# A fused conv and SwiGLU stack on one core: a two-element variance step moves from ScalarE to VectorE, under a new order of steps

## Chip, cores and metric

One core of a Trainium2 chip runs the whole kernel. The metric is device microseconds (us) of one execution, the median of several runs of the compiled program; lower is better.

## The reference

The input `x` is 2048 rows by 512 features in bf16. Four blocks follow one another, A, B, A, B, each behind a layernorm and each added back to `x`:

```python
x = A_q
x = x + _A_ref(_layernorm(x), A_k, A_v, A_shift_k, A_ssm_k, A_ssm_D)   # conv block
x = x + _B_ref(_layernorm(x), B_w_gate, B_w_up, B_w_down)              # SwiGLU FFN
x = x + _A_ref(_layernorm(x), ...)                                     # same weights again
x = x + _B_ref(_layernorm(x), ...)

def _layernorm(x, axis=-1, eps=1e-5):
    m = jnp.mean(x, axis=axis, keepdims=True); v = jnp.var(x, axis=axis, keepdims=True)
    return (x - m) / jnp.sqrt(v + eps)
# _A_ref: kv = (4-tap causal shift conv of k) * v;  y = causal long conv of kv with ssm_k over
#         the 2048 positions (by FFT) + kv * ssm_D;  returns q * y, with q the normalised x
# _B_ref: (silu(q @ w_gate) * (q @ w_up)) @ w_down, 512 -> 1792 -> 512
```

The conv's output `y` does not depend on `x`, so both layers use the same `y`.

## The kernel before

The 2048 rows are cut into 4 chunks of 512 rows, and each chunk into 2 halves of 256 rows. A *unit* (layer, chunk, half) is one pass of one half through one layer: its prologue and its FFN. There are 16 units. The conv is computed chunk by chunk as DFT blocks on TensorE with spectral products on VectorE, and is interleaved with the FFNs of the units.

The **prologue** of a unit is a chain over four engines:

1. statistics of the layernorm of `x`, then `rstd = (var + eps) ** -0.5` on GpSimd (POOL), in `power()`, L891: one `tensor_tensor` with `pow` over 128x2 values. It is called here *the power step*. There are 32 of them, two in each prologue.
2. `n = (x - m) * rstd` (`normalise`, on VectorE L952 or ScalarE L947), `n *= y` (L974), `x += n` (L975), both on VectorE
3. statistics of the new `x`, the second power step, `z` normalised (L952 or L947), transposed by DMA into `zT` (L982). The FFN of the unit begins on TensorE when `zT` is there.

The statistics come in two forms. `ln_stats` uses VectorE: `bn_stats` (L900) and `bn_aggr` (L901) into `mv`; 20 of the 32 power steps read `mv`. `ln_stats_act` uses ScalarE for the sums: two `Square` activations with an accumulated sum (L924) into `sm`, then a small `Identity` activation (L928) that makes `ve = sm / D + eps` of 128x2 values; 12 of the 32 power steps read `ve`. Where ScalarE also normalises, a pair of tiny ScalarE steps (L940) or one of VectorE (L936) makes `nmr = -mean * rstd` first.

The **FFN** of a unit runs on TensorE: gate and up products into four PSUM banks `pf` (L402 in the profile, issued at L1109 and L1164), each evacuated by ScalarE (Silu into `sg`, L1111 and L1171; a cast into `hr` or `ht`, L1112 and L1175), multiplied on VectorE (L1118, L1178), transposed by DMA where the rows lie the other way (L1120), then the down product into `pd` (L1198), evacuated by ScalarE into `dn` (L1243, L1246) and added to `x` by VectorE (L1250).

The order of everything is fixed. The kernel first makes a list of 1721 steps with `add(engine, cost, emit, reads, writes, ...)`. The table `ORDER` gives each step of that list its place in one overall sequence; each engine issues its own steps in that sequence and waits on semaphores where a step needs another engine's result. A step therefore holds up everything behind it on its engine. Rings of buffers are given out along that sequence too (`pf` has 4).

Of the kernel before, what the change touches and what calls it, by code (L numbers as in the profile page):

```python
# [9 lines left out]
P = 128  # L10
F32 = mybir.dt.float32
# [3 lines left out]
ALU = mybir.AluOpType  # L15
# [314 lines left out]
def kernel(  # L330
# [58 lines left out]
    def whole(name, shape, dtype=BF16, parts=1):  # L389
        return new("one", name, shape, dtype, parts)  # L390
# [1126 lines left out]
```

## Time and profile before

| | |
|---|---|
| median of 3 runs | 341.59 us (341.46 to 341.8) |
| the profiled execution | 341.52 us, of which the span is 339.7 us |
| granted TensorE clock | 1.00 |
| busy, TensorE / VectorE / ScalarE / GpSimd | 333.5 / 299.7 / 264.2 / 35.5 us |
| instructions on the same | 2172 / 507 / 544 / 48 |
| power steps fed by `mv` (VectorE) | 20, mean 835 ns |
| power steps fed by `ve` (ScalarE) | 12, mean 1268 ns |
| ScalarE's step that makes `ve` | 12, mean 298 ns |

The span is the stretch that the profile covers; the time of an execution is 1.8 us longer. Busy time of TensorE counts a matmul to its modelled end, so idle TensorE time shows best as a gap between the starts of two matmuls.

### The profile page before, as it was taken

Reading aid. Unit: us, or ns where it says so; the run is one execution under the profiler, and the core shown is the slowest. Engines: PE = TensorE matmul, PEld = TensorE weight load, DVE = VectorE, ACT = ScalarE, POOL = GpSimd, SP = SyncE. Lnnn points to the kernel's source line nnn. Section 1 sums busy time; section 2 is a strip of 40 time slices with the busy share of each in tenths; the row PEclk is TensorE's granted clock in tenths of the full one; section 3 lists DMA queues with packets and bytes.
Section 4 is the critical chain, followed back from the end, with each engine's and each line's share of the span. In section 5 each row is a group of like instructions: output and inputs, shape, how many; then the busy total and the mean of one; then the engine's idle time right before and its main releaser. Section 6 shows DMA issues by size and latency. Waiting matters only on the chain.

```text
span 339.7 us, 5935 instructions
## 1 busy us (share of the span) xinstructions
PE 333.5 (98%) x2172; PEld 204.9 (60%) x2172; DVE 299.7 (88%) x507; ACT 264.2 (78%) x544; POOL 35.5 (10%) x48
## 2 busy tenths in 40 slices
PE   9999999799999999999999999999999999999996
PEld 7766864544545564745445464654546587858884
DVE  7899999799788999999999999999998887966465
ACT  7999999698996675979899985989675547465373
POOL 4000112303010100102110100002001000100000
PEclk9999999999999999999999999999999999999999
DMA  7999602251417445382324244420504430123011
GB/s 271 339 294 367 122 8 56 51 127 39 94 31 96 93 108 125 62 147 59 62 43 83 46 92 127 93 48 3 105 17 94 65 78 11 39 48 77 2 34 62
DMA packets 77992, 31.59 MB, mean 93 GB/s; under 512 B 69765, under 2 KB 75786, under 8 KB 77962
## 3 DMA queue, kind: packets, MB, share of 16 engines
q1 hardware_dynamic: 77808, 31.13, 39.5%
q8 instruction: 17, 0.28, 0.3%
q14 instruction: 13, 0.11, 0.1%
q10 hardware_dynamic: 154, 0.07, 0.1%
HBM read 12.33 MB, written 2.10 MB: 42 GB/s over the span
## 4 chain that ended last, share of the span: by engine, by line
PE 89%; DVE 5%; ACT 3%; POOL 1%; DMA 1%; issue 1%
PE pf L402 54%; PE pd L1198 20%; PE ps L1073 7%; PE ps L402 6%; POOL rstd L891 1%; DVE t L734 1%; PE wm L1483 1%; DVE Z L738 1%; DMA sg<-hr 1%; DVE m L875 1%; PE pt L569 0%; DVE bst L900 0%; ACT jk L924 0%; DVE G L537 0%; ACT sg L1111 0%
## 5 line engine op out<-in xcount | busy, mean ns | idle before, releaser
L402 PEld LDWEIGHTS <-zT 128*128 128x128 bf16 x528 | 51.5, 98 | 60.6 <-DMA zT<-z 1.0
L402 PE MATMUL pf<-wu_sb,zT 128*128 128x512 bf16 x264 | 65.3, 379 | 0.0
L402 PE MATMUL pf<-wg_sb,zT 128*128 128x512 bf16 x264 | 65.2, 379 | 0.0
L1198 PE MATMUL pd<-wd_sb,sg 128*128 128x512 bf16 x200 | 49.3, 379 | 0.1
L402 PE MATMUL pf<-zT,wu_sb 128*128 128x256 bf16 x368 | 46.1, 272 | 1.8 <-ACT sg L1111 1.6
L1111 ACT ACTIVATE sg<-pf 128x512 bf16<-128x512 f32 x66 | 39.2, 611 | 10.0 <-PE pf L402 8.3
L402 PE MATMUL pf<-zT,wg_sb 128*128 128x256 bf16 x368 | 46.1, 273 | 0.0
L1112 ACT CAST hr<-pf 128x512 bf16<-128x512 f32 x66 | 38.1, 598 | 8.6 <-PE pf L402 7.8
L402 PEld LDWEIGHTS <-wu_sb 128*128 128x128 bf16 x368 | 36.0, 98 | 9.8 <-issue 2.6
L744 DVE TENSOR_TENSOR t<-X,G 128x4096 bf16<-128x4096 bf16 x18 | 41.1, 2285 | 0.0
L402 PEld LDWEIGHTS <-wg_sb 128*128 128x128 bf16 x368 | 36.0, 98 | 7.3
L1175 ACT CAST ht<-pf 128x512 bf16<-128x512 f32 x46 | 26.8, 598 | 12.1 <-PE pf L402 10.1
L1198 PEld LDWEIGHTS <-sg 128*128 128x128 bf16 x200 | 19.4, 98 | 22.3 <-DMA sg<-hr 1.0
L891 POOL TENSOR_TENSOR rstd<-mv,nhalf 128x2 f32<-128x2 f32 x20 | 16.7, 835 | 150.5 <-DVE mv L901 139.5
L1171 ACT ACTIVATE sg<-pf 128x512 bf16<-128x512 f32 x46 | 27.1, 614 | 6.5 <-PE pf L402 5.7
L1198 PE MATMUL pd<-wd_sb,ht 128*128 128x512 bf16 (+1 forms) x126 | 29.9, 369 | 0.0
L891 POOL TENSOR_TENSOR rstd<-ve,nhalf 128x2 f32<-128x2 f32 x12 | 15.2, 1268 | 121.5 <-ACT ve L928 121.5
L900 DVE BATCH_NORM_STATS2 bst<-xc 128x6 f32<-128x512 bf16 x40 | 26.5, 683 | 0.6
L1178 DVE TENSOR_TENSOR ht<-ht,sg 128x512 bf16<-128x512 bf16 (+1 forms) x31 | 16.6, 546 | 9.4 <-ACT ht L1175 7.5
L1118 DVE TENSOR_TENSOR hr<-hr,sg 128x1024 bf16<-128x1024 bf16 x27 | 18.5, 685 | 5.3 <-ACT sg L1111 3.0
L511 ACT ACTIVATE X<-ps 128x512 bf16<-128x512 f32 x32 | 19.1, 614 | 1.5 <-PE ps L402 0.9
L1198 PEld LDWEIGHTS <-ht 128*128 128x128 bf16 x126 | 12.3, 98 | 12.2 <-ACT z L947 0.2
(143 smaller groups left out, 528.3 us busy)
## 6 DMA issues: line engine op xcount, KB each, us to landing
hn<-in_A_ssm_k_dram SPq DMA_DIRECT2D x4, 512.0 KB, 6.0
vt<-in_A_v_dram SPq DMA_DIRECT2D x4, 512.0 KB, 8.8
xc<-in_A_q_dram SPq DMA_DIRECT2D x4, 512.0 KB, 5.4
out_dram<-xc SPq DMA_DIRECT2D x15, 128.0 KB, 1.8
wg_sb<-in_B_w_gate_dram SPq DMA_DIRECT2D x1, 1792.0 KB
wu_sb<-in_B_w_up_dram SPq DMA_DIRECT2D x1, 1792.0 KB, 7.9
wd_sb<-in_B_w_down_dram SPq DMA_DIRECT2D x1, 1280.0 KB
sg<-hr SPq DMA_TRANSPOSE x66, 2.4
```

Source lines behind the costliest of these rows:

```text
L402: nc.tensor.matmul(o, lhsT=lhsT, rhs=rhs, start=(n == 0), stop=(n == len(terms) - 1))
L511: add("ACT", act(D), lambda: nc.scalar.activation(out=view(), in_=ps.t[:], func=ACT.Copy, scale=scale), r=[ps], w=[(buf, keys)], conv=conv)
L744: dve(8 * D, lambda t=t, part=part: nc.vector.tensor_mul(out=t.t[:], in0=x.t[:, :, part:part + 1, :].to_broadcast((P, R, 2, D)), in1=g.t[: ...
L891: add("POOL", cost, lambda: nc.gpsimd.tensor_tensor(out=rstd.t[:], in0=var(), in1=nhalf.t[:].to_broadcast((P, n)), op=ALU.pow), r=reads + ...
L900: add("DVE", 0.6, lambda st=st, i=i: nc.vector.bn_stats(out=st.t[:, 0:6], in_=xs[c].t[:, i, :]), r=[(xs[c], (i,))], w=[st])
L1073: nc.tensor.matmul(bank.t[:, half_ * C:(half_ + 1) * C], lhsT=lhsT(i), rhs=rhs(i), start=(first and i == 0 and half_ == 0), stop=(last and ...
L1111: add("ACT", act(D), lambda ps=ps, dst=dst, o=o, which=which: nc.scalar.activation(out=rows(dst, o), in_=ps.t[:], func=ACT.Silu) if which ...
L1112: out=rows(dst, o), in_=ps.t[:], func=ACT.Silu) if which == "g" else nc.scalar.copy(out=rows(dst, o), in_=ps.t[:]),
L1118: dve(n * W, lambda: nc.vector.tensor_mul(out=hr.t[:], in0=hr.t[:], in1=sg.t[:]), [sg], [hr], due=(unit, k / pairs, 0.0, "h"))
L1171: add("ACT", act(D), lambda ps=ps, o=o, sg=sg: nc.scalar.activation(out=sg.t[:, o:o + 2, :], in_=ps.t[:], func=ACT.Silu), r=[ps], w=[(sg, ...
L1175: add("ACT", act(D), lambda ps=ps, o=o, ht=ht: nc.scalar.copy(out=ht.t[:, o:o + 2, :], in_=ps.t[:]), r=[ps], w=[(ht, (o // 2,))], due=(uni ...
L1198: nc.tensor.matmul((pds[o] if not cs.start else pds[HP]).t[:, cs], lhsT=ht.tiles(q, o), rhs=wt["d"].t[:, ft, cs], start=(ft == std0 and no ...
```

## The change

`ve` is no longer made by ScalarE with an activation whose bias is a tile holding eps, but by VectorE with one `tensor_scalar` (multiply by 1/D, add eps). The tile `eps` and the GpSimd memset that filled it go away, so there are 1720 steps, and every power step now reads a value that VectorE wrote. The table `ORDER` is another permutation throughout.

```diff
@@ ORDER: all 1721 entries replaced by 1720 others @@
-    6, 53, 44, 124, 2, 7, 4, 12, 24, 1, 3, 0, 17, 18, 30, 10, 8, 11, 9, 15, 27, 21, 19, 16, 20, ...
+    4, 44, 184, 2, 0, 1, 6, 20, 7, 8, 14, 16, 17, 18, 5, 3, 9, 10, 12, 26, 15, 21, 13, 19, 22, ...
...
-    eps = whole("eps", [P, 1], F32)
...
         ve = new("ve", "ve", [P, n], F32)
-        add("ACT", TINY, lambda: nc.scalar.activation(out=ve.t[:], in_=sm.t[:, n:2 * n], func=ACT.Identity, scale=1.0 / D, bias=eps.t[:]),
-            r=[(sm, range(n, 2 * n)), eps], w=[ve])
+        add("DVE", 0.08, lambda: nc.vector.tensor_scalar(out=ve.t[:], in0=sm.t[:, n:2 * n], scalar1=1.0 / D, scalar2=LN_EPS,
+                                                         op0=ALU.mult, op1=ALU.add), r=[(sm, range(n, 2 * n))], w=[ve])
         return nm, power(lambda: ve.t[:], [ve], n, PWA)
...
-    add("POOL", 0.1, lambda: nc.gpsimd.memset(eps.t[:], LN_EPS), w=[eps], due=-47)
```

What the new table says on VectorE around four of the places that the prediction speaks of (`VE` is the new step; each list is the order of issue):

| prologue | before | after |
|---|---|---|
| unit (0,0,0), first power step | ..., L537, L539, L537, L734, L734, L734, L738, ... | ..., L537, L539, L734, L734, `VE`, L738, L734, ... |
| unit (1,0,0), first power step | L920, L1250, L649, L649, L748, L744, L1118, L744, L1118, L974 | L920, L1250, L748, L649, L638, `VE`, L638, L649, L1118, L744, L1118, L901, L974 |
| unit (1,1,1), first power step | L920, L1250, L900, L744, L748, L1118, L748, L974 | L920, L1250, L744, `VE`, L744, L1118, L748, L974 |
| unit (1,1,1), second power step | L974, L975, L901, L900, L900, L901, L901, L1118, L952, L936 | L974, L975, L1118, L900, L900, L901, L901, L748, L936 |

128 rows, old and new, of the table ORDER are left out of this document.

## The prediction

> **What bounds the kernel now.** The page comes first, for the engine that is never idle, then the stages, for where it is idle after all.
>
> ```profile
> PE 333.5 (98%) x2172; PEld 204.9 (60%) x2172; DVE 299.7 (88%) x507; ACT 264.2 (78%) x544; POOL 35.5 (10%) x48
> ```
>
> ```profile
> 30.00:40.00 10.00, 9.41 (x90) 7.78 (x88) 9.52 (x16) 9.53 (x26) 1.64 (x2) 1.00 0.99 245
> 50.00:60.00 10.00, 10.00 (x52) 4.95 (x51) 9.96 (x13) 9.85 (x22) 2.42 (x1) 1.00 0.27 54
> 60.00:70.00 10.00, 8.20 (x57) 5.33 (x56) 7.50 (x12) 7.32 (x15) 3.38 (x2) 1.00 0.33 66
> 190.00:200.00 10.00, 10.00 (x60) 5.69 (x59) 9.97 (x14) 9.71 (x18) 1.40 (x1) 1.00 0.32 66
> ```
>
> The columns are the stretch, its length, then busy time of PE, PEld, DVE, ACT and POOL, the granted clock and DMA. TensorE is full nearly everywhere at clock 1.00. The change takes nothing from TensorE, so it can only gain what TensorE waits for, and the one large hole lies at 60 to 70 us. The chain of waits names its cause, and the timeline shows it at work:
>
> ```profile
> 57.21 0.30 ACT ve L928
> 57.59 5.04 POOL rstd L891
> 62.65 0.30 ACT nmr L940
> ```
>
> ```profile
> 56.98 2.28 DVE L744 TENSOR_TENSOR t<-X,G 128x4096 bf16<-128x4096 bf16 x1
> 57.59 5.03 POOL L891 TENSOR_TENSOR rstd<-ve,nhalf 128x2 f32<-128x2 f32 x1 [10.93 <-ACT ve L928]
> 59.18 0.69 DVE L1118 TENSOR_TENSOR hr<-hr,sg 128x1024 bf16<-128x1024 bf16 x1
> 59.78 2.29 DVE L744 TENSOR_TENSOR t<-X,G 128x4096 bf16<-128x4096 bf16 x1
> 62.57 0.38 PE L402 MATMUL ps<-hs,fwd 128*128 128x512 bf16 x1
> 64.51 1.03 PE L402 MATMUL pf<-zT,wu_sb 128*128 128x256 bf16 x8 [1.56 <-ACT sg L1111]
> 65.69 1.03 PE L402 MATMUL pf<-zT,wu_sb 128*128 128x256 bf16 x8 [0.15 <-ACT sg L1171]
> 66.56 3.01 PE L1198 MATMUL pd<-wd_sb,sg 128*128 128x512 bf16 x12
> ```
>
> This is the first power step of unit (1,0,0). ScalarE released it in the middle of a VectorE product (56.98 to 59.26); it came through only 0.55 us after VectorE had fallen idle at 62.07, past two boundaries between instructions. ScalarE stood at nmr until 62.65, the Silu evacuations behind that were late, and TensorE ran out of `pf` banks.
>
> In full flow a 512-column matmul starts every 0.215 us and a 256-column one every 0.109, as the rows of 12 and 8 show with their last matmul's 0.38 and 0.27 taken off. By that, TensorE waited 64.51 - 62.57 - 0.21 = 1.73, then 65.69 - 64.51 - 0.87 = 0.31, then 0.25 inside the row of 12: **2.3 us**.
>
> **The change part by part.**
>
> ```profile
> L891 POOL TENSOR_TENSOR rstd<-mv,nhalf 128x2 f32<-128x2 f32 x20 | 16.7, 835 | 150.5 <-DVE mv L901 139.5
> L891 POOL TENSOR_TENSOR rstd<-ve,nhalf 128x2 f32<-128x2 f32 x12 | 15.2, 1268 | 121.5 <-ACT ve L928 121.5
> L928 ACT ACTIVATE ve<-sm,eps 128x2 f32<-128x2 f32 x12 | 3.6, 298 | 0.2
> L920 DVE SCALAR_TENSOR_TENSOR nm<-sm,mv 128x2 f32<-128x2 f32 x4 | 0.6, 156 | 0.3 <-ACT dn L1246 0.3
> L1263 POOL MEMSET eps<- 128x1 f32 x1 | 0.1, 93 | 0.0
> 45.46 0.65 DVE L1178 TENSOR_TENSOR ht<-ht,sg 128x1024 bf16<-128x1024 bf16 x1
> 45.62 1.03 POOL L891 TENSOR_TENSOR rstd<-mv,nhalf 128x2 f32<-128x2 f32 x1 [6.36 <-DVE mv L901]
> 46.02 2.28 DVE L744 TENSOR_TENSOR t<-X,G 128x4096 bf16<-128x4096 bf16 x1
> ```
>
> *Removed:* twelve ScalarE steps, 12 x 0.298 = 3.6 us, and a memset of 0.09 us that nobody waits for. Both lie beside TensorE's work: zero on the path, and a loss is excluded; a gain is the first rival.
>
> *Added:* twelve VectorE steps. The nearest row is L920, of the same 128x2 values: 12 x 0.156 = 1.9 us of VectorE, beside TensorE's work except in the start.
>
> *The power step itself.* A power step released by VectorE is not free of VectorE. At 45.46 VectorE had already gone on to its next instruction when the step started at 45.62; the step ended at 46.65, 0.54 us after that instruction (46.11), although a 2.28 us product followed at 46.02. So it waits for one VectorE instruction, whichever the order puts behind the trigger, and then gets through. Behind `mv` in the old order that instruction is short, hence the mean of 835 ns.
>
> The Trainium skill says the same more sharply (SBUF — State Buffer, "Who interferes with whom"): an instruction of VectorE with two SBUF inputs and one of GpSimd that reads SBUF exclude each other, and the first to issue blocks the other for its whole length. That speaks against this change, since VectorE now always issues first. By that rule the step at 57.59 would have come free at 59.26; the trace has 2.8 us more.
>
> *Unit (1,0,0).* In the new table the 0.69 us L638 follows the new step, so the power step should take about 1.0 as at 45.62, where it took 5.03. VectorE's other work ahead of L974 is no longer than before. The 2.3 us go, and next late is nothing: the chain that made `zT` too late becomes about 4 us shorter, more than TensorE waited. **-2.3 us.**
>
> *Start.* The first VE step stands in a VectorE chain that ends in TensorE's waits before the first FFN (0.6 us in the 30 to 40 row). It adds 0.156 us there, and up to 0.3 if it waits for ScalarE's square: **+0.2 us**.
>
> *Unit (1,1,1).* Here the new table puts a 2.28 us product (L744) right behind the new step.
>
> ```profile
> 150.72 1.03 PE L402 MATMUL pf<-wu_sb,zT 128*128 128x512 bf16 x4
> 151.43 0.16 DVE L920 SCALAR_TENSOR_TENSOR nm<-sm,mv 128x2 f32<-128x2 f32 x1 [0.34 <-ACT dn L1246]
> 154.69 0.84 POOL L891 TENSOR_TENSOR rstd<-ve,nhalf 128x2 f32<-128x2 f32 x1 [11.74 <-ACT ve L928]
> 155.64 0.59 ACT L1112 CAST hr<-pf 128x512 bf16<-128x512 f32 x1
> 156.76 1.22 DVE L748 TENSOR_TENSOR t<-t,t 128x2048 bf16<-128x2048 bf16 x1
> 158.04 0.69 DVE L974 TENSOR_TENSOR n<-n,Yk 128x1024 bf16<-128x1024 bf16 x1
> 160.93 0.69 DVE L1118 TENSOR_TENSOR hr<-hr,sg 128x1024 bf16<-128x1024 bf16 x1
> 161.16 1.66 POOL L891 TENSOR_TENSOR rstd<-mv,nhalf 128x2 f32<-128x2 f32 x2 [1.15 <-DVE mv L901]
> 162.20 0.16 DVE L936 SCALAR_TENSOR_TENSOR nmr<-mv,rstd 128x2 f32<-128x2 f32 x1 [0.26 <-POOL rstd L891]
> 162.41 1.50 ACT L947 ACTIVATE z<-xc,nmr,rstd 128x512 bf16<-128x512 bf16 x2
> 166.68 1.03 PE L402 MATMUL pf<-wu_sb,zT 128*128 128x512 bf16 x4
> ```
>
> ```profile
> sg<-hr SPq DMA_TRANSPOSE x66, 2.4
> ```
>
> I count from 150.72, where TensorE begins unit (1,1,0). Before: L920 at 0.7, power step done at 4.8, L974 at 7.3, nmr at 11.5, first z done at 12.5 (half of the 1.50), `zT` 2.4 later at 14.9, used at 16.0.
>
> After: L920 at 0.7, L1250 (0.69) and one L744 (2.28) ahead of the new step, which so starts at 3.6; the second L744 runs from 3.7 to 6.0, the power step ends at 6.5 (+0.55). From there to L974 the rows have 2.5, of which ScalarE spent 0.5 finishing a cast; ScalarE is free now: L974 at 8.5. Up to nmr the rows have 4.2; the new order adds an L1118 in this stretch (0.6 from start to start) and has the L748 (1.22) behind the trigger where the L1118 (0.69) was, but nothing is late ahead of it otherwise: 8.5 + 4.2 + 0.6 + 0.5 = 13.8 to 13.9. First z done at 14.9, `zT` at 17.3.
>
> In the new table TensorE has work ahead of that place worth 76 matmuls of 512 columns (two of 256 counted as one), 76 x 0.216 = 16.4 us, and nothing to fill the rest. It waits 17.3 - 16.4 = 0.9. ScalarE moreover stands at the first nmr until 6.5, with `pf` evacuations of unit (1,1,0) behind it, as in unit (1,0,0); for that I add 0.2, the smaller of the two bank waits there being 0.31: **+1.1 us**. Lower bound 0, if z comes a microsecond sooner; upper bound 1.1 + 1.8 (below).
>
> *The other prologues* I have not counted step by step. I take 0, up to +0.6, the size of the other hole above (10.00 - 9.41). GpSimd's own steps are reordered too, but it stands idle for nine tenths of the span.
>
> **Sum**, against the profiled execution: 341.52 - 2.3 + 0.2 + 1.1 = 340.5; the median of the runs lies 0.07 higher: **340.6 us**.
>
> **The rivals.**
>
> *The whole gain (339.5).* Unit (1,1,1)'s chain keeps up, because ScalarE, 3.6 us lighter, evacuates earlier. For it: the 1.1 us rest on a margin of the same size. Against: its chain waits for VectorE and GpSimd. 341.6 - 2.3 + 0.2 = 339.5.
>
> *The power step of (1,1,1) is passed over again (342.4).* At 57.59 the step waited 1.7 us for the first boundary and missed it and the next; the longest wait of a step that got through at the first boundary is this one's, 1.40 less 0.55:
>
> ```profile
> 191.37 1.40 POOL L891 TENSOR_TENSOR rstd<-ve,nhalf 128x2 f32<-128x2 f32 x1 [14.16 <-ACT ve L928]
> ```
>
> Behind the L744 it would wait 2.1. If it misses two boundaries as there, it comes free when VectorE stands still ahead of L974, after the L1118 and L748 (0.6 + 1.2 later): +1.8, so 340.6 + 1.8 = 342.4. It decides as soon as one L744 behind a trigger is enough to lose the boundary. By the page cited above, which frees the step with the instruction that was first, it couldn't happen; the step at 57.59 says otherwise.
>
> *The new steps stop VectorE (343.1).* Each VE step waits for ScalarE's squares, and queued behind it stand the products that feed TensorE (L1118, L1178) and the conv's L744 to L752. The L920 row above shows such a wait, 0.34 us; 0.34 + 0.16 = 0.5 a step. VectorE has no slack in stretches like 50 to 60 and 190 to 200 (9.96 and 9.97 of 10), and I take 5 of the twelve to fall into such: +2.5, so 340.6 + 2.5 = 343.1. It decides when these waits exceed 1 us together. Against: the table places most new steps behind one or two long VectorE instructions after the squares.
>
> *It doesn't do what it says (341.8).* The chain of (1,0,0) is as late as before for another reason, such as the transposes that the new order moves in SP's queue: 341.6 + 0.2 for the start.
>
> **How the numbers follow.** Forecast 340.6 (its own range 339.9 to 341.3): 0.38. Whole gain: 0.16. Passed over again: 0.17. VectorE stopped: 0.18. Nothing gained: 0.11. Less than 0.2% (0.68 us) either way is what a measurement of this kernel can't tell from no change; same is 340.9 to 342.3. Faster: 0.16 and 0.27 of the forecast's 0.38. Same: 0.11 of the forecast's and 0.06 of nothing gained. Slower: the rest, 0.40. For 8 in 10 the range runs from 339.3 to 343.0.
>
> **What would show it.** Right: twelve VectorE steps of about 0.16 us and no L928; the power step of (1,0,0) near 1 us; no hole at 60 to 70 us; a power step of 2.6 to 2.8 us behind an L744 near 155 us and a TensorE gap of about 1 us near 165. A power step of over 4 us there means the second rival; idle time of VectorE put down to ScalarE's accumulators of several microseconds the third. Wrong altogether would be a new hole of TensorE at a place named nowhere here.

## The result and the profile after

The changed kernel takes 347.68 us (median of 6 runs, 345.72 to 347.94), the kernel before 341.55 in the same runs: a ratio of 1.0164, 95% interval 1.0138 to 1.0190. The profiled execution took 347.60 us, 345.8 of them its span. It is slower by 6.1 us, where the prediction had 1 us faster and a range up to 343.0.

The page of the changed kernel, its first line, and the two groups of power steps further down (line numbers are one lower than before, since one line went; 30 records of matmuls are missing from this trace, hence 2142 beside 2172):

```profile
PE 334.9 (97%) x2142; PEld 206.4 (60%) x2172; DVE 300.5 (87%) x519; ACT 263.0 (76%) x532; POOL 40.0 (12%) x47
L890 POOL TENSOR_TENSOR rstd<-mv,nhalf 128x2 f32<-128x2 f32 x20 | 19.7, 987 | 163.4 <-DVE mv L900 157.1
L890 POOL TENSOR_TENSOR rstd<-ve,nhalf 128x2 f32<-128x2 f32 x12 | 16.4, 1373 | 110.3 <-DVE ve L927 110.3
```

The power steps on `ve`, which the change was to free, are longer than before (mean 1373 ns, was 1268). Two of the twelve make up more than half of the group. The chain of waits shows both, with what follows them:

```profile
56.98 4.48 POOL rstd L890
61.48 0.49 ACT nmr L939 x2
...
156.63 4.34 POOL rstd L890
161.00 0.48 ACT nmr L939 x2
```

The timeline of VectorE and GpSimd around the first one, unit (1,0,0), and of TensorE behind it:

```profile
56.74 0.17 DVE L927 TENSOR_SCALAR ve<-sm 128x2 f32<-128x2 f32 x1
56.81 0.69 DVE L637 TENSOR_TENSOR X<-m 128x1024 bf16<-128x1024 bf16 x1
56.98 4.47 POOL L890 TENSOR_TENSOR rstd<-ve,nhalf 128x2 f32<-128x2 f32 x1 [9.74 <-DVE ve L927]
57.41 0.69 DVE L648 TENSOR_TENSOR X<-m 128x1024 bf16<-128x1024 bf16 x1
58.01 0.69 DVE L1117 TENSOR_TENSOR hr<-hr,sg 128x1024 bf16<-128x1024 bf16 x1
58.61 2.29 DVE L743 TENSOR_TENSOR t<-X,G 128x4096 bf16<-128x4096 bf16 x1
60.24 0.93 PE L402 MATMUL pf<-zT,wu_sb 128*128 128x256 bf16 x7
63.34 4.00 PE L402 MATMUL pf<-zT,wg_sb 128*128 128x256 bf16 x21 [2.18 <-ACT sg L1110]
```

The short L637 does stand behind the new step, as the prediction had read from the table, and it ends at 57.50. The power step does not come through there, nor at the next two boundaries between products: it is *passed over*, as this is called below. It ends at 61.45, 0.55 us after VectorE ran out of work at 60.90. TensorE then stands still from 61.0 to 63.34: 2.34 us between one start and the next that was due. And the row of 21 behind it takes 4.00 us. In full flow 21 matmuls of 256 columns take 20 x 0.109 + 0.27 = 2.45, so another 1.55 us went there. The same in unit (1,1,1):

```profile
156.32 0.16 DVE L927 TENSOR_SCALAR ve<-sm 128x2 f32<-128x2 f32 x1
156.39 2.28 DVE L743 TENSOR_TENSOR t<-X,G 128x4096 bf16<-128x4096 bf16 x1
156.63 4.33 POOL L890 TENSOR_TENSOR rstd<-ve,nhalf 128x2 f32<-128x2 f32 x1 [9.10 <-DVE ve L927]
158.59 0.68 DVE L1117 TENSOR_TENSOR hr<-hr,sg 128x1024 bf16<-128x1024 bf16 x1
159.20 1.22 DVE L747 TENSOR_TENSOR t<-t,t 128x2048 bf16<-128x2048 bf16 x1
163.42 1.87 PE L402 MATMUL pf<-wu_sb,zT 128*128 128x512 bf16 x4 [2.42 <-ACT sg L1110]
165.07 1.71 PE L402 MATMUL pf<-wg_sb,zT 128*128 128x512 bf16 x4
```

This hole is 2.58 us long, and four matmuls of 512 columns then take 1.87 and 1.71 us instead of 1.03. The table by stretches names the reason; behind the five engines its third column from the end is the granted clock. Its first two rows are the start:

```profile
20.00:30.00 10.00, 9.63 (x86) 6.06 (x86) 9.82 (x23) 9.79 (x20) 0.00 (x0) 1.00 1.04 352
30.00:40.00 10.00, 9.56 (x92) 7.80 (x92) 9.59 (x17) 10.00 (x25) 1.63 (x2) 1.00 1.02 234
...
64.00:66.00 2.00, 2.00 (x12) 1.45 (x10) 1.93 (x5) 2.00 (x4) 0.00 (x0) 0.51 0.14 33
66.00:68.00 2.00, 1.95 (x11) 1.37 (x11) 1.52 (x4) 0.84 (x3) 0.37 (x1) 0.64 0.44 98
164.00:166.00 2.00, 2.00 (x7) 0.68 (x5) 1.97 (x4) 1.40 (x3) 0.00 (x0) 0.50 0.00 0
```

Around the end of each of the two holes TensorE's granted clock was halved for about 3.4 us. In the profile before, the hole of 1.73 us was not followed by that (1.00 in all rows). So the 6.1 us: TensorE's holes, (2.34 + 2.58) in place of 2.3; the start, 0.8 of waits from 20 to 40 us in place of 0.6 (10.00 and 9.41 before); some tenths elsewhere; and 1.55 + 0.84 + 0.68 = 3.1 us at half clock. That is 2.6 + 0.2 + 3.1 = 5.9. This holds for the profiled execution. The one of the six runs whose granted clock was 1.00 still took 346.21 us, only 1.4 us less than the profiled one at 0.99, so about half of the 3.1 us is not saved where the clock stays full; what stands in its place there no trace shows.

### The profile page after: what moved, and what is told of

Same layout as the page of the kernel before. It is cut to its first block, busy times and chain, and to the rows that moved or that the text cites. A ratio compares the mean times of both kernels' runs of the same rounds, so it can differ in the third digit from the quotient of the medians.

```text
span 345.8 us, 5896 instructions
## 1 busy us (share of the span) xinstructions
PE 334.9 (97%) x2142; PEld 206.4 (60%) x2172; DVE 300.5 (87%) x519; ACT 263.0 (76%) x532; POOL 40.0 (12%) x47
## 4 chain that ended last, share of the span: by engine, by line
PE 74%; DVE 14%; ACT 5%; POOL 3%; DMA 2%; issue 2%; DVEq 0%; ACTq 0%; POOLq 0%
PE pf L402 44%; PE pd L1197 16%; PE ps L1072 7%; PE ps L402 5%; POOL rstd L890 3%; DVE t L743 2%; DVE m L631 2%; DVE t L733 1%; PE wm L1481 1%; DMA zT<-z 1%; ACT X L510 1%; DVE bst L899 1%; ACT sg L1110 1%; DVE ht L1177 1%; DVE Z L737 1%
## 5 line engine op out<-in xcount | busy, mean ns | idle before, releaser
L402 PE MATMUL pf<-zT,wg_sb 128*128 128x256 bf16 x368 | 48.2, 279 | 2.2 <-ACT sg L1110 2.2
L1197 PE MATMUL pd<-wd_sb,sg 128*128 128x512 bf16 x194 | 47.3, 379 | 0.4
L402 PEld LDWEIGHTS <-wg_sb 128*128 128x128 bf16 x368 | 36.8, 100 | 11.2 <-issue 3.2
L890 POOL TENSOR_TENSOR rstd<-mv,nhalf 128x2 f32<-128x2 f32 x20 | 19.7, 987 | 163.4 <-DVE mv L900 157.1
L890 POOL TENSOR_TENSOR rstd<-ve,nhalf 128x2 f32<-128x2 f32 x12 | 16.4, 1373 | 110.3 <-DVE ve L927 110.3
L510 ACT ACTIVATE X<-ps 128x512 bf16<-128x512 f32 x32 | 18.4, 603 | 0.9 <-PE ps L549 0.7
```

The costliest lines, as they stand in the source:

```text
L402: nc.tensor.matmul(o, lhsT=lhsT, rhs=rhs, start=(n == 0), stop=(n == len(terms) - 1))
L510: add("ACT", act(D), lambda: nc.scalar.activation(out=view(), in_=ps.t[:], func=ACT.Copy, scale=scale), r=[ps], w=[(buf, keys)], conv=conv)
L890: add("POOL", cost, lambda: nc.gpsimd.tensor_tensor(out=rstd.t[:], in0=var(), in1=nhalf.t[:].to_broadcast((P, n)), op=ALU.pow), r=reads + ...
L1197: nc.tensor.matmul((pds[o] if not cs.start else pds[HP]).t[:, cs], lhsT=ht.tiles(q, o), rhs=wt["d"].t[:, ft, cs], start=(ft == std0 and no ...
```

## Experiments

Ratios are to the kernel before, in the same runs, with 95% intervals. Theory A was that the two passed-over power steps, their holes and the clock behind them make the loss; theory B, that the new orders do.

**The two steps given a way through.** One bn_stats of 0.69 us, with one input and a result that nobody reads, is put on VectorE behind the new step: in both units, or in one. The edit in short:

```
         ve = ...  add("DVE", 0.08, tensor_scalar(out=ve, ...))
+        if len(plan.ops) in PAD:          # (1,0,0), (1,1,1) or both
+            add("DVE", 0.69, bn_stats(out=junk, in_=xs[c][:, rows[0], :]))
```

> The kernel after, with one bn_stats of 0.69 us (one input, result unused) put on VectorE right behind the new VE step of units (1,0,0) and (1,1,1), so that both power steps have a non-blocking instruction to get through beside. Theory A (the 6.1 us are two TensorE holes of 2.34 and 2.58 us, each followed by about 3 us at half clock that cost 1.7 us, and both holes come from power steps that were passed over): both power steps near 0.7 us, no hole over 0.7 us, granted clock 1.00 behind 60 us, time 347.6 - 8.3 + 0.2 = 339.5 (339.2 to 340.2), which is under both kernels. Theory B (the new orders cost the time by themselves, the power steps only happen to be late beside it): 346 or more.

> As above with the bn_stats in unit (1,0,0) alone. Theory A: the hole at 61 us and its half clock go, the other stays: 347.6 - 2.34 - 1.7 = 343.6 (343.2 to 344.2). Theory B: 346 or more. If the clock falls by chance and not by the hole, the time differs from run to run by 1.7 us.

> As above with the bn_stats in unit (1,1,1) alone. Theory A: the hole at 161 us and its half clock go, that at 61 us stays: 347.6 - 2.58 - 1.7 = 343.3 (342.9 to 344.0). Theory B: 346 or more.

Measured: both 341.26 us (1.0001, 0.9989 to 1.0013); (1,0,0) alone 343.10 (1.0057, 1.0036 to 1.0077); (1,1,1) alone 344.61 (1.0090, 1.0057 to 1.0123), which is over the range that A gave. With both, the two power steps take 0.69 us each and TensorE's two holes are gone; here is (1,0,0):

```profile
56.24 0.69 DVE L928 BATCH_NORM_STATS2 junk<-xc 128x6 f32<-128x512 bf16 x1
56.41 0.69 POOL L890 TENSOR_TENSOR rstd<-ve,nhalf 128x2 f32<-128x2 f32 x1 [9.74 <-DVE ve L927]
```

The loss goes with the two steps, each by its share, and theory B falls. But 341.26 is 1.8 us over what A said. Of these, 1.0 us stands between 180 and 230 us, where TensorE was full before (50.00 of 50 us) and is busy for 49.04 here: two other `ve` steps were passed over, of 3.87 and 2.20 us. The first of them, in the profile of the kernel with both:

```profile
189.44 0.42 DVE L1114 TENSOR_TENSOR hr<-hr,sg 128x512 bf16<-128x512 bf16 x1
189.68 3.87 POOL L890 TENSOR_TENSOR rstd<-ve,nhalf 128x2 f32<-128x2 f32 x1 [8.82 <-DVE ve L927]
189.78 0.68 DVE L637 TENSOR_TENSOR H<-m 128x1024 bf16<-128x1024 bf16 x1
190.38 0.42 DVE L1177 TENSOR_TENSOR ht<-ht,sg 128x512 bf16<-128x512 bf16 x1
190.71 2.29 DVE L743 TENSOR_TENSOR t<-X,G 128x4096 bf16<-128x4096 bf16 x1
```

In the changed kernel the same step, with the same instructions behind it, had taken 0.73 us. What lies behind a step does not settle by itself whether it gets through.

The runs of the half-padded kernels also price the clock: their granted clock is about 0.995 in some runs and 1.00 in the others, and these differ by 1.6 us with the hole of (1,0,0) left (345.57 and 345.28 against 343.93 and 343.64), by 0.9 with that of (1,1,1) (343.97 and 344.03 against 343.04 to 343.10). A hole of 2.3 to 2.6 us is followed by the half clock in some executions and not in others.

**Many steps at known places.** The edit in short:

```
+    for i in range(37):                   # ahead of 37 chosen VectorE instructions
+        add("DVE",  tensor_scalar(out=pv, in0=t0, mult 1/D, add eps))
+        add("POOL", tensor_tensor(out=pr, in0=pv, in1=nhalf, pow))
```

> The kernel after with 37 additional pairs on constants: a VE-like step of 0.16 us on VectorE and a power step on GpSimd that it releases, each pair ahead of a chosen VectorE instruction (products of 2.28 us, halves of 1.22, 0.69 and 0.42). Their results are not used. Theory 1 (a step that has waited over some 1.2 us misses the boundary): the power steps ahead of 1.22 us or less take that length plus 0.55 less 0.25 (1.5 us at most), nearly all of those ahead of 2.28 us products take over 3 us. Theory 2 (what follows decides, or chance): steps of 4 us and more appear behind short instructions as often as behind long ones. The prediction's rule (one VectorE instruction, then through): none over 2.7 us. The time itself, some microseconds longer, says nothing.

Measured: 11 of the 37 were passed over, 9 of them behind instructions of 1.22 us or less. Theory 1 falls: a step behind a 2.28 us product got through at the first boundary, another behind the same pair of products did not:

```profile
128.16 4.49 DVE L743 TENSOR_TENSOR t<-X,G 128x4096 bf16<-128x4096 bf16 x2
128.40 2.60 POOL L1478 TENSOR_TENSOR pr<-pv,nhalf 128x2 f32<-128x2 f32 x1 [5.72 <-DVE pv L1477]
...
174.27 4.49 DVE L743 TENSOR_TENSOR t<-X,G 128x4096 bf16<-128x4096 bf16 x2
174.50 7.01 POOL L1478 TENSOR_TENSOR pr<-pv,nhalf 128x2 f32<-128x2 f32 x2 [3.20 <-DVE pv L1477]
178.67 0.17 DVE L1477 TENSOR_SCALAR pv<-t 128x2 f32<-128x2 f32 x1
```

(The row of 7.01 holds two steps; the first took 4.81 and ended 0.56 us after the second product, where a VectorE instruction with one input came.) The prediction's rule falls too, but a new one shows: no step on `mv` was passed over.

**The layout.** `mv` holds its variances 8 bytes apart, `ve` side by side.

```
-        ve = new("ve", "ve", [P, n], F32)      # written and read as ve.t[:]
+        ve = new("ve", "ve", [P, n, 2], F32)   # written and read as ve.t[:, :, 1]
```

> The kernel after with one change: `ve` is laid out like `mv`, two values 8 bytes apart (a tile of 128 x 2 x 2, its second column written and read), where it was two adjacent values. In all traces so far no power step on `mv` was ever passed over at a boundary between two products, and about half of those on two adjacent values (ve, and the additional pairs) were. Theory L (the layout read by the power step decides): no step is passed over; (1,0,0) takes about 1.06 us, (1,1,1) 2.6 us, 196 us 0.73, and the time is the one first predicted or a little less, 339.3 to 341.0. Theory T (what decides is something that goes with the trigger or the phase, not the layout): of the twelve ve steps two to four still take over 3.5 us, and the time is 343 to 348.

> The 37 additional pairs at the same places, their two values laid out 8 bytes apart like `mv`. Theory L: none is passed over at a boundary (where 12 of them were with adjacent values); the longest takes about 2.7 us. Theory T: about as many are passed over as before, 8 to 14. The kernel's own ve steps keep their adjacent values and may still be passed over.

Measured: 347.63 us (1.0183, 1.0168 to 1.0198), (1,0,0) 4.47 and (1,1,1) 4.33 us; of the pairs the same 11 were passed over, at the same places (the count of 12 in the expectations was one too many). Theory L falls. Nor is it chance alone, since two programs with the same order agree in every step that is passed over.

**Half of the change each.** The new orders with `ve` on ScalarE, and the old orders with `ve` on VectorE.

```
order_alone: kernel before,  ORDER = the new table (with a place for the memset of eps)
edit_alone:  kernel after,   ORDER = the old table (without that place)
```

> The new orders with ve computed on ScalarE as before (the memset of eps kept). If the new orders by themselves were the loss: 346 or more with all power steps under 2.7 us. By the theory of the passed-over steps the time goes with the steps: with both of (1,0,0) and (1,1,1) let through, 340 to 342; for each one that is passed over and leaves a hole of 2.3 to 2.6 us, 2.5 to 4.2 more.

> The old orders with ve computed on VectorE, each step at the old place in the sequence. There VectorE would reach the new step of (1,0,0) at 54.7 and the squares are done at 57.2; that of (1,1,1) at 152.2 for 154.3, two more at 230.0 for 232.1 and 237.7 for 239.9, so VectorE stops four times for over 2 us each. Expected: slower than before by one to four microseconds (342.5 to 346), with idle time of VectorE put down to ScalarE's squares; the power step of (1,0,0) has a 0.69 us product behind it and would take 1.0 us or be passed over until VectorE's next idle time. If VectorE's idle time costs nothing: 339 to 340.

Measured: order_alone 349.20 us (1.0234, 1.0210 to 1.0259), both steps passed over (4.28 and 4.43 us) although ScalarE released them, and one more hole of 1.80 us at 244 us, where the down product waited for a transpose (`sg<-hr`). edit_alone 348.22 us (1.0202, 1.0187 to 1.0218), more than I had expected. There the power step of (1,0,0) takes 1.06 us, but the waits of VectorE read:

```profile
DVE ve L928 <- ACT jk L924: 9.4, 5, 2.4
```

9.4 us of standing before five new steps, the longest 2.4 us. So the old order does not suit the new step, and neither half is good alone.

**A wait for the own last result.** Ahead of every `mv` power step stands a bn_aggr, which reads what VectorE itself wrote, in most of them just before. The new step is given the same: two instructions, the second reading the first.

```
-        ve <- sm * 1/D + eps
+        ve' <- sm * 1/D + eps ;  ve <- ve' * 1 + 0
```

> The kernel after with each new VE step made in two VectorE instructions, the second (times 1, plus 0) reading what the first wrote, as bn_aggr reads what bn_stats wrote: 12 x 0.2 us more of VectorE. Theory Q (a power step is passed over where VectorE's queue behind the trigger stands ready, and gets through where VectorE had to wait for its own last result just before, as it always has behind bn_aggr): no ve step is passed over, (1,0,0) takes about 1.06 us and (1,1,1) 2.6 us, the two holes shrink to under 1 us, time 339.5 to 341.5. Theory T (something else in the order or in the phase): (1,0,0) or (1,1,1) or both still over 4 us, time 343 to 348.

> The 37 additional pairs at the same places, their VectorE part made of two instructions, the second reading what the first wrote. Theory Q: none of the 37 passed over at a boundary between two products (12 of 37 were, with one instruction or with the strided layout). Theory T: 8 to 14 of them.

> The kernel after with a bn_stats of 0.69 us (result unused) behind four of the twelve VE steps: (1,0,0), (1,1,1) and the two whose power steps took 3.87 and 2.20 us with the first two padded (near 190 and 218 us). If these two late steps are what is left of the loss (TensorE holes of 0.3 to 0.5 us at 189, 209, 218 and 222 us, 1.7 us together): 341.3 - 1.7 + 0.2 = 339.8 (339.4 to 340.4), under both kernels. If VectorE's additional work is the limit by then: 341 or more.

Measured: ve_chain 341.64 us (0.9994, 0.9974 to 1.0014), a little over the range given, with a hole of 1.26 us left in (1,1,1). Theory Q holds in both: no `ve` step and none of the 37 pairs was passed over. Here is (1,1,1) of ve_chain, then the pair ahead of the two products at which the single instruction had failed:

```profile
153.28 0.16 DVE L927 TENSOR_SCALAR ve<-sm 128x2 f32<-128x2 f32 x1
153.47 0.17 DVE L927 TENSOR_SCALAR ve<-ve 128x2 f32<-128x2 f32 x1
153.55 2.29 DVE L743 TENSOR_TENSOR t<-X,G 128x4096 bf16<-128x4096 bf16 x1
153.78 2.60 POOL L890 TENSOR_TENSOR rstd<-ve,nhalf 128x2 f32<-128x2 f32 x1 [9.51 <-DVE ve L927]
155.76 0.68 DVE L1117 TENSOR_TENSOR hr<-hr,sg 128x1024 bf16<-128x1024 bf16 x1
```

```profile
176.37 0.16 DVE L1477 TENSOR_SCALAR pv<-t 128x2 f32<-128x2 f32 x1
176.56 0.17 DVE L1477 TENSOR_SCALAR pv<-pv 128x2 f32<-128x2 f32 x1
176.64 4.48 DVE L743 TENSOR_TENSOR t<-X,G 128x4096 bf16<-128x4096 bf16 x2
176.88 2.60 POOL L1478 TENSOR_TENSOR pr<-pv,nhalf 128x2 f32<-128x2 f32 x1 [4.54 <-DVE pv L1477]
```

pad_four took 341.62 us (1.0008, 0.9996 to 1.0021): all four steps come through, but TensorE has a new wait of 1.12 us at 218.6 us, where the last of the 0.69 us instructions was put, and the gain did not come.

**Dependence or length.** 

> The 37 additional pairs at the same places with two VectorE instructions ahead of each power step, as in the chained ones, but both reading the constant, so that the second waits for nothing. Theory Q (the wait for the own last result keeps the following products from standing ready): about as many passed over as behind a single instruction, 8 to 14. If the second short instruction is what matters: none or one.

Measured: 13 passed over. The second instruction by itself does nothing; it is the wait that the dependence makes. The three groups of 37 side by side, single, paired and chained, each from its own kernel:

```profile
L1478 POOL TENSOR_TENSOR pr<-pv,nhalf 128x2 f32<-128x2 f32 x37 | 67.6, 1833 | 97.4 <-DVE pv L1477 97.4
```

```profile
L1478 POOL TENSOR_TENSOR pr<-pv,nhalf 128x2 f32<-128x2 f32 x37 | 71.2, 1931 | 96.4 <-DVE pv L1477 96.4
```

```profile
L1478 POOL TENSOR_TENSOR pr<-pv,nhalf 128x2 f32<-128x2 f32 x37 | 47.2, 1277 | 122.6 <-DVE pv L1477 122.6
```

**The hole of the kernel before.** One VectorE instruction on one column is put at the first boundary that the step at 57.59 was passed over at. In after_doors the like stands in three places, with the bn_stats in (1,1,1).

```
   t  <- X * G         L744, 2.28 us, runs when ScalarE releases the power step
+  door <- nhalf * 1 + 0   128x1, one input, result unused
   hr <- hr * sg       L1118
```

> The kernel before with a single additional VectorE instruction (one column of 128 values, one input, result unused) between the product L744 and the L1118 behind it in unit (1,0,0): the first boundary that the power step at 57.59 was passed over at. If what holds the step is the queue of ready two-input products, whoever released it, it gets through there: about 2.2 us in place of 5.03, TensorE's 2.3 us go, time 341.5 - 2.3 + 0.1 = 339.3 (339.0 to 340.0). If the step was late for another reason (ScalarE's release, or TensorE's wait had another cause behind it): 341 or more.

> The kernel after with such a one-column instruction behind the first product that follows the VE step in three places ((1,0,0), and the steps near 190 and 218 us), and the bn_stats behind the VE step of (1,1,1). All four power steps under 1.2 us. If VectorE's additional 0.69 us instructions were what kept the padded kernels at 341.3 to 341.6: 339.6 to 340.4. If the new orders lose by themselves what they gain elsewhere (starts, waits of 0.2 to 0.5 us near 210 to 225 us): 341.0 to 341.6 again.

Measured: before_door 338.91 us, 0.9929 (0.9916 to 0.9943), against 339.3 expected; after_doors 340.89, 0.9983 (0.9972 to 0.9995), between its two ranges, with all four steps under 1.2 us. The timeline of before_door, and its stretch from 60 to 70 us, where the kernel before had 8.20:

```profile
56.64 2.28 DVE L744 TENSOR_TENSOR t<-X,G 128x4096 bf16<-128x4096 bf16 x1
57.26 2.22 POOL L891 TENSOR_TENSOR rstd<-ve,nhalf 128x2 f32<-128x2 f32 x1 [10.94 <-ACT ve L928]
58.84 0.14 DVE L1477 TENSOR_SCALAR door<-nhalf 128x1 f32<-128x1 f32 x1
58.91 0.68 DVE L1118 TENSOR_TENSOR hr<-hr,sg 128x1024 bf16<-128x1024 bf16 x1
```

```profile
60.00:70.00 10.00, 10.00 (x67) 6.30 (x65) 9.90 (x14) 9.82 (x19) 0.77 (x1) 1.00 0.42 83
```

The power step takes 2.22 us in place of 5.03, and the hole is gone. A single instruction of 0.14 us gives what the change was after, without it, and this version is the fastest of all. That it was ScalarE that released the step was not the trouble. In after_doors TensorE still waits 0.4 us from 180 to 230 us, in place of 1.0 with the bn_stats alone; so the late steps there were part of the 1.8 us, not all.

## Why the prediction was wrong, step by step

The change did what it says: twelve VectorE steps of about 0.16 us, no `ve` on ScalarE.

**The power step of (1,0,0), -2.3 us, is the step that failed.** "So it waits for one VectorE instruction, whichever the order puts behind the trigger, and then gets through" was read from steps on `mv`. The one step of the kernel before that broke the rule (57.59) I put down to a ScalarE release in the middle of a product, and did not ask whether the rule held for a trigger that VectorE makes without waiting for itself. All traces of this case together show more. I count every power step that found a VectorE instruction with two inputs running and had another such one overlapping behind it:

- Steps on `mv`: 120 came through at that first boundary, none was passed over.
- `ve` or additional pairs behind two dependent instructions: 36 came through, none was passed over.
- All others, released by ScalarE or by an independent VectorE instruction: 92 came through, 58 were passed over. These 58 met 66 more boundaries between two products and were passed over at all of them. 29 came out when VectorE stood still, 29 where an instruction with one input came, 0.55 to 0.56 us after the end of the product ahead.

Which of the 150 are passed over stays open. In 41 of the 92, VectorE had just stood still: the product that was running, or the instruction ahead of it, had begun less than 0.06 us before the end of its predecessor, where 0.07 to 0.11 us is usual. In none of the 58 had it. So the wait need not be for VectorE's own result: in edit_alone three of these steps follow a `ve` that waited 2.07 to 2.37 us for ScalarE, and all three came through. Nor is a wait needed by every step: 14 of the 120 on `mv` follow a bn_aggr that ran straight behind an unrelated product, as here in the kernel before, where L1118 ran from 78.34 to 78.99 and L638 started at 78.90:

```profile
77.13 1.18 DVE L632 TENSOR_TENSOR m<-Z 128x2048 bf16<-128x2048 bf16 x1
78.23 0.19 DVE L901 BATCH_NORM_AGGREGATE mv<-bst 128x2 f32<-128x9 f32 x1
78.57 0.97 POOL L891 TENSOR_TENSOR rstd<-mv,nhalf 128x2 f32<-128x2 f32 x1 [9.56 <-DVE mv L901]
```

What lets those in, no run here tells. Products that stand ready one behind the other would explain the steps that are passed over, and a VectorE that has just waited has none ready. But the trace does not show its queue, so that is argued, not shown.

**Unit (1,1,1), +1.1 us.** The mechanism of the second rival came in full: "A power step of over 4 us there means the second rival", and it took 4.33. Its hole is 2.58 us where that rival had 1.1 + 1.8 = 2.9. Where the step did come through at the first boundary (ve_chain, 2.60 us against the 2.6 to 2.8 predicted), the hole was 1.26 against 1.1. The sum of that unit was sound; only the rule in it was wrong.

**The half clock, 3.1 us in the profiled execution, was foreseen nowhere.** I took a microsecond of waiting for a microsecond of time, because the hole of 1.73 us in the profile before had cost just that. With the second rival taken for (1,0,0) too, the sum would have been 341.5 + 2.9 + 0.2 = 344.6, still 3 us short.

**The start, +0.2:** 0.2 by the stretches. **The other prologues, 0 to +0.6:** nothing over 0.35 us in the changed kernel. But there the steps near 190 and 218 us happened to come through; in other versions of it they did not.

**The third rival,** VE steps that stop VectorE, did not come in the changed kernel, whose table had been made for it, and came under the old table (edit_alone, 9.4 us of VectorE standing). Which of TensorE's waits there come from it, I have not followed.

**The rule of the Trainium skill.** The Trainium skill (SBUF — State Buffer, "Who interferes with whom") says that the one that issues first holds the shared ports to SBUF, the memory in which these tiles lie, for its whole instruction and the other blocks. By that, (1,0,0) would have come free at 57.50; the trace has 60.90. A further sentence there, that a VectorE instruction with at most one SBUF input, outside its two-port modes, does not contend with GpSimd, agrees with the traces: 29 steps came out at an instruction with one input, and one of 0.14 us was enough; the modes no trace shows.

The new table itself may have followed the same rule. The planner's own model of the step, in the function `walk` of the kernel, lets it end with the VectorE instruction that was running:

```
                if n >= 0 and vec[n].two and vec[n].end > o.start:
                    settle(vec[n].end)
```

A table searched under this model sees no harm in a line of products behind the trigger. That the search used it is what the code suggests; no run here tried another.

## What to carry to other kernels

Where GpSimd reads SBUF while VectorE runs two-input instructions back to back, a GpSimd step may not get in until VectorE has a gap or a one-input instruction. In these runs it always got in at the first boundary where VectorE had just stood still at the trigger, and making the trigger wait for VectorE's own last result was enough for that. A one-column copy at the right boundary costs 0.14 us and here gained 2.5. Before moving the producer of a late step, look at what the step waits for after it is released. And price a TensorE hole of over 2 us at up to 1.6 us more than its length, for the half clock that may follow.

## What the runs showed of the hardware

- A GpSimd step that misses its first boundary between two two-input VectorE instructions missed all later ones, 66 of 66.
- TensorE's granted clock was halved for about 3.4 us (matmuls of 256 columns starting every 0.213 us instead of 0.109, from 64.0 to 67.5 us) after holes of 2.34 and 2.58 us, in some executions; in the profile before it did not follow the hole of 1.73 us. It may at times: one of 19 runs of the kernel before, beside ve_chain, took 344.49 us at a granted clock of 0.995, the others 341.03 to 342.30 at 0.999 or 1.00; no trace of that run is kept. The Trainium skill (TensorE: Matmul & The Clock Gate, "What's actually happening") has the clock fall after at least one idle window of about 3.4 us, a free-running one. The 3.4 us at half clock and the change from one execution to the next fit that; but holes a quarter to a third shorter than that window were enough here.
